# Exp tiles in column blocks of 64, one mask per unit, corner copies of V by DMA, a new order

## The chip, the cores and the metric

One core of a Trainium2 chip runs the whole kernel: TensorE (PE; PEld are its weight loads), VectorE (DVE), ScalarE (ACT), GpSimd (POOL), and SyncE (SP), which only issues DMAs here. The metric is the device time of one execution in microseconds (us); the comparison is between medians of executions.

## What is computed

Two layers, each an attention with memory (32 heads of width 16, 2,048 tokens in 4 segments of 512, causal inside a segment) and a gated feed-forward block, all in bfloat16:

```python
for s in range(N):                        # 4 segments
    logits = einsum('bhqd,bhkd->bhqk', qs, ks) * scale + mask   # causal, 512 x 512
    a_dot = einsum('bhqk,bhkd->bhqd', softmax(logits), vs)
    a_mem = (phi(qs) @ M) / (phi(qs) @ z + 1e-06)
    outs.append(g * a_mem + (1.0 - g) * a_dot)
    M, z = M + phi(ks)^T vs, z + sum(phi(ks))
x = x + A(layernorm(x)); x = x + (silu(n @ w1) * (n @ w3)) @ w2   # n = layernorm(x); twice
```

## The kernel before

The program is a list of some 3,700 operations with their dependencies. `ORDER` is a written-out permutation of their numbers; every engine runs its operations in that order and waits for the semaphores of what they depend on. `OTHER` lists the operations that take the second of two possible engines: evictions of PSUM (`ev`, L520 on ScalarE, L521 on VectorE), scalings (`km`, `ke`), sums of heads (`oadd`). There are 8 segments (4 in each layer). The attention of one segment is interleaved with the feed-forward of earlier ones and the projections of later ones.

**Logits.** The heads go in 4 groups G of 8; `ee` is the even or the odd head of a pair, and four pairs lie side by side in the array's four strips of 32 rows. One logits unit (`lg`, L984) fills 512 columns of four PSUM banks. A block `("f", G, ee, j, ...)` of a unit is row tile j (128 keys) against the queries it can see, less the first 64: widths 448, 320, 192 and 64. Those first 64 queries of each row tile (the own corner) are done for both heads at once in units of `("s", ...)` blocks. Matmuls of a unit come in groups of four, one for each strip, that run side by side. A logits unit needs row tiles; the other matmuls run with the whole array or with column tiles, and `quarters` (L233) writes a full matmul as four column tiles where it stands among attention products.

**Exp and masks.** One Exp (L1000) turns the four banks into a tile `e` of [128, 4 strips, 512]. Where a row tile meets its own diagonal, GpSimd zeroes what is above it (`affine_select`, L1009): in an `f` unit one instruction for each row tile, 128 x 256 elements; in an `s` unit four of 1,024.

**Attention product.** `attend` (L1056) multiplies V by these tiles, in four column strips; `f` blocks read V from `va`, the corners from `vj`, a copy of V with the odd heads shifted by 64 partitions (L787, two copies on VectorE for a segment, four in segment 0). There is one `vj` buffer (`VJ = 1`). The result is evicted (`evX`, tile `xs`), transposed by DMA on SyncE (L1070), normalised, and transposed back (L1101).

**The head.** Segment 0 is done in two halves, with Exp tiles of two strips. While it runs, segment 1's tokens are normalised on VectorE (L691), turned on TensorE (`flip`, L701, four flips) and evicted (L521, `W`), and segment 1's projections wait for that.

```python
for n, b in enumerate(own):
    cut(("f", n), 64, lambda ebuf=ebuf, c=b[4]: e_r[ebuf.slot][:, :, c:c + 64], [[0, 4], [1, 64]], 256)
```

Of the kernel before, what the change touches and what calls it, by code (L numbers as in the profile page):

```python
# [3 lines left out]
ACT = mybir.ActivationFunctionType  # L4
# [4 lines left out]
P = 128  # L9
# [3 lines left out]
NCG = 4  # L13
# [239 lines left out]
def o_pe(ns):  # L253
# [7 lines left out]
    27 5 30 29 0 32 31 34 33 9 35 10-13 21 2 23 1 14 36-37 44 38-39 6 15 26 45-46 16-20 40 47 41-42 48 43 49 55 54  # L261
    51 50 52 3 53 78 4 7 79 102 90 57 91-92 103-104 22 80 58 85 81-82 93 86 74 56 68 8 59-60 83 67 87-88 64 69 105
    89 94 106-110 186 96 188 187 189 61 95 97 190 111 98 191 99-100 113-114 101 84 115-119 192 120 112 121 202-203
    62 127 677 194 673 65 196 70 122-123 66 193 195 212 128 63 675 71 154 678 134 197 135-136 210 137-138 213 25
    198 200 204 76 671-672 211 139 205 140-141 199 155 124 142 129 674 156 125 143 157 201 676 130 215 158 369 159
    131 160 145 161 126 72 208 162 146 228-229 147-152 174 179-180 216 165 153 132 679 73 226 260 181-182 680 166
    175 167-168 372 370 214 227 163 261 231 373 133 218-219 362 258 176-177 266 183 217 232 259 169 687 170-172 690
    684 242 178 691 209 230 268 267 233 173 371 685 269 243 144 262 24 688 164 220 206 681 686 184 250 185 274 682
    263 251-252 275 689 272 270 1122 276-277 375 743 207 273 264 744 683 234 271 265 280 278 288-289 748-749 1120
    750-751 692 709 235 1118-1119 752 286 281 287 284 1121 710-711 253 285 712 745-746 244 1116-1117 726 279 727  # L270
    282 747 298 1123 374 376 1124 713 254-255 290 1125 704 728 283 256 300 257 705-706 299 301 308 28 729 693 221
    304 222 224 714 245 303 309-310 730 694 291 695 311 707 312 708 236 696 313 306-307 302 305 314 324 223 1127
    380 325 315 322 698 323 292 699 720 697 328 330-331 721 700 225 327 701 246 237 1126 1128 760 1129-1130 238 329
    326 248 722 702 1131 715-718 247 75 719 761 381 723 348 336 338 731 239 753 724 240 316 754 337 346 898 764 339
    377 349 732 755 334 733 378 703 763 249 734 762 756 347 382 735 1132-1133 332 351 241 335 738 333 340 1168
    1134-1135 293-294 765 1136 739 353 352 740-741 296 295 297 1169 777 1170-1171 900 383 317 742 384 1142 901 385
    318 778 757 1172 1143 350 320 319 341 321 354-355 737 902 356 781 904 1144 758 1145 1147 379 1146 782 779 736
    1163-1164 783 1148 386 1165 1149 780 342-343 367 759 77 387 1150 785 1185 388 897 389 1186 1151 784 1187 899
    390-391 903 1188 393 392 395 1166 786 1175 795 344 396 345 394 1189 787 1158 766 1159-1160 767-768 1167 789
    1176-1177 1161 796 1162 908 771 791 1197 909 1180-1181 790 1178 772 1190 1182 1191 1183 792 1192-1193 1198  # L280
    397-398 357-361 1179 1337 801 1137 1199 400 1153 399 788 793 1138-1139 401 1154 1194 797 1184 1155 802
    1156-1157 775 1140 366 776 1338 1141 799 905-906 805 794 773 769 800 407-408 798 402 774 806 770 403 809 421
# [12 lines left out]
    544 1600 890 1223 1195 1209 875 1579 1336 1601-1603 876-877 1580-1582 545 1590 1583 1224 1228 891-892 894 893
    1595-1596 551 1604 629-632 1591 1229 1597 895 1598 633-634 1599 896 1220 1226 635 1569 636-637 1570 1225 1232
    1571 1592-1594 1217 1212 1227 1233 1617 1572-1573 1618-1620 1238-1239 1621 1230 1213 1635 921 1978 926-928
    922-925 1236 1242 929 1237 1627 1234-1235 916 1638 930 1976 1605 917-919 1606-1607 1243 920 935 933 1608-1609
    1255 911 1231 1340 912-913 1240-1241 936 914 659 937 915 1628 1347 931 938 1256 1246 1629 1259 1247 1637
    647-648 934 1342-1343 649-651 932 1245 660 1258 1244 939-940 1248 661 1210-1211 662-666 1260 944 942 941 1257  # L300
    1261 1634 652 1262 943 1265-1266 945 1268 1263 667-668 1264 653-654 669 1249 1273 670 1274 1269-1270 1574-1575
    1636 1250 1576-1577 655-657 1630 1578 1982 1251-1252 1639 1584 1282 1977 1344 1631 1271 946-948 1253 658
    1585-1587 1283 952-953 1588 949 954 950-951 955 1288 1286 1980 1640 1284-1285 1289 1272 964 956 1641 965
    958-960 1642 966 1275 967 961 970 1292 968-969 1979 971-973 981 962 1287 963 974 1622-1623 982-983 1643 1276
    1293 1644 1294 1624-1625 1267 1983 1981 1984 984 1626 985 1985 1298 986 957 987 1299 1589 1295-1297 975 1987
    976-977 1277 1291 978-979 1279 1019 980 1302-1303 1989 1020 997-999 1021 988-989 1990 1003 1278 1305 1986 1022
    1000 1315 1004 1301 1290 1005 1254 990 1001 1316 991 1300 1317 1006 1002 1610 992-993 1007 1991 994-995 1306
    1319 1307 1014 1023 1015-1017 996 1611 1018 2057 1008-1010 1320 1988 1321 1011 2007 1012 1651 2008 1024 1013
    1322 1652 2009-2010 1308 1992 2018 1318 1993 2019 1280 1994-1995 1325 1655 1281 1304 1656 2011 1323 1996 1326
    1025 2020-2022 1997-1999 1026 1324 2000 1659-1660 1657 1030 1309-1310 1312 2028-2031 1633 1653 1327 1311 1654  # L310
    2001 1027 1031 1052 1032 1658 1033-1034 1313 2032 1665 1028 1661 1053 1035 2035-2037 1663 1029 2175 1054-1055
    1666 1314 2038 1036 1328-1329 2002-2004 1331 2174 2005-2006 1667 2039 1669 1664 1330 1037-1040 1670 1672
    1332-1333 2050 1662 2051-2054 1041-1042 1675 1632 1668 1047-1048 1056-1057 2045 1043 2046 2177 2047-2049 1676
    2013-2014 2176 2180 2015 1044-1045 2016-2017 1673 1049 1679-1680 1671 1674 1046 2040-2043 1050 2044 1058-1061
    2023 1677 1692-1693 2178-2179 1051 1062 1683 1363-1364 2033 1684 2181 2024-2025 1365 1358 2026-2027 1366-1367
    1694 2012 1696 1359-1361 1678 1362 1348-1349 1697 1353-1356 1374 1698 1357 1682 1350 1702 1375 1649 1068 1650
    1351 1699 1352 1685 1063 1695 1370 1069 1703 1681 1064-1065 1372-1373 1700 1371 1104 1070 1701 1705 1066 1706
    1105 1067 1368 1106-1107 1071-1074 1369 1710 1686 1376 1075-1076 1711 1108 1707 1077 1719-1720 1092-1093 1109
    1645 1377 1704 1110 1721 1379 1378 1380-1381 1078 1111 1646 1112 1079 1094 1725 1709 1726 2034 1113 2182-2183
# [103 lines left out]
def build(nc, A_x, A_wq, A_wk, A_wv, A_wo, A_beta, B_w1, B_w3, B_w2, out):  # L423
# [66 lines left out]
    def vpairs(t, i):  # L490
        return t[:, i, 0:VS * H].rearrange("p (e h c) -> p h e c", e=2, c=VS)

    def vcol(G, pg, ee):
        return VS * (16 * ee + 4 * G + pg)
# [415 lines left out]
    def unit_list(part):  # L910
# [5 lines left out]
        if part == (0, LT):  # L916
            for G in range(NCG):
# [3 lines left out]
                if G % 2 == 0:  # L921
                    out.append((share, [(G, 0)]))
# [363 lines left out]
```

## Time and profile before

| | us |
|---|---|
| median of 3 executions | 474.56 |
| lowest and highest | 474.35, 476.81 |
| the profiled execution | 477.68 |
| its span, first to last instruction | 475.9 |
| TensorE busy in the span | 461.8 |

A busy share is an average over the span; what ends a stretch is read from the timelines. A matmul's duration in the rows includes its way through the array, so distances between starts tell its cost.

### The profile page before, as it was taken

What the parts mean: (1) busy time and instruction counts of PE and PEld (TensorE: products, weight loads), DVE (VectorE), ACT (ScalarE), POOL (GpSimd) and SP (SyncE); (2) the same over time, 40 slices, a digit from 0 to 9 for tenths busy, and PEclk for the clock granted to TensorE, in tenths of its full rate; (3) what the DMA queues carried; (4) which work ended last, traced back from release to release, by engine and by line L of the source; (5) the groups of instructions that cost most, each with busy time, mean ns of one, the idle gap of its engine ahead of it and who ended that gap; (6) DMA issues with size and microseconds to landing.
All of it is one profiled execution on the core that took longest, in us unless ns stands there. A gap on an engine that the chain in (4) does not pass through costs nothing.

```text
span 475.9 us, 19641 instructions
## 1 busy us (share of the span) xinstructions
PE 461.8 (97%) x8757; PEld 237.7 (50%) x8793; DVE 388.8 (82%) x843; ACT 380.9 (80%) x362; POOL 242.3 (51%) x418
## 2 busy tenths in 40 slices
PE   8989989999999999999999999999999999999997
PEld 4544446764554444544545444454444444454554
DVE  7887998988999888798888788697795778688673
ACT  5969989999999897989888999889898887560230
POOL 3973376655565644757364533746563565550000
PEclk9979999999999999999999999999999999999999
DMA  7744637643243332281235531542315332531402
GB/s 233 273 101 59 90 72 139 155 60 68 49 77 62 68 61 37 41 113 29 45 68 70 79 68 23 68 93 45 59 25 86 28 47 46 91 81 36 102 1 69
DMA packets 105780, 35.92 MB, mean 75 GB/s; under 512 B 98816, under 2 KB 104064, under 8 KB 105696
## 3 DMA queue, kind: packets, MB, share of 16 engines
q1 hardware_dynamic: 104016, 31.41, 36.0%
q0 software_dynamic: 720, 2.46, 1.8%
q8 instruction: 69, 1.13, 1.0%
q10 hardware_dynamic: 960, 0.79, 0.5%
q14 instruction: 15, 0.12, 0.1%
HBM read 8.43 MB, written 2.10 MB: 22 GB/s over the span
## 4 chain that ended last, share of the span: by engine, by line
PE 85%; DVE 9%; ACT 3%; issue 1%; DMA 1%; POOL 0%; DVEq 0%; POOLq 0%
PE psall L228 34%; PE psall L233 33%; PE psall L984 9%; PE psall L1056 7%; ACT e L1000 2%; DVE W L521 1%; DVE xn L691 1%; DVE va L521 1%; DVE W L831 1%; DVE W L833 1%; DVE ln L672 1%; DMA x_tok<-in_A_x_dram 1%; PE psall L856 0%; DVE vj L787 0%; DVE xs L521 0%
## 5 line engine op out<-in xcount | busy, mean ns | idle before, releaser
L1000 ACT ACTIVATE e<-psall 128x2048 bf16<-128x2048 f32 (+1 forms) x162 | 272.0, 1694 | 37.3 <-PE psall L984 30.9
L1009 POOL TENSOR_SCALAR_AFFINE_SELECT e<-e 128x256 bf16<-128x256 bf16 (+2 forms) x320 | 175.2, 572 | 149.8 <-ACT e L1000 78.5
L228 PE MATMUL psall<-W,w 128*128 128x512 bf16 (+1 forms) x382 | 84.8, 352 | 0.1
L233 PE MATMUL psall<-W,w 128*32 128x512 bf16 (+1 forms) x1352 | 79.0, 361 | 0.0
L1177 DVE SCALAR_TENSOR_TENSOR gp<-th,psall 128x512 bf16<-128x512 bf16 x80 | 53.8, 681 | 12.0 <-ACT th L1175 11.4
L1181 DVE SCALAR_TENSOR_TENSOR h<-gp,psall 128x512 bf16<-128x512 bf16 x80 | 54.0, 681 | 10.7 <-PE psall L228 6.3
L1175 ACT ACTIVATE th<-psall 128x512 bf16<-128x512 f32 x80 | 47.2, 604 | 16.6 <-PE psall L233 13.8
L233 PE MATMUL psall<-w,h 128*32 128x512 bf16 (+3 forms) x916 | 54.7, 370 | 0.0
L228 PEld LDWEIGHTS psall<-W,w 128*128 128x128 bf16 x382 | 34.5, 98 | 34.5 <-issue 5.3
L233 PEld LDWEIGHTS psall<-W,w 128*32 128x32 bf16 x1352 | 33.7, 97 | 25.8 <-issue 1.7
L672 DVE BATCH_NORM_STATS2 ln<-x_tok 128x6 f32<-128x512 bf16 x64 | 42.8, 682 | 1.3 <-DMA x_tok<-in_A_x_dram 1.0
L984 PE MATMUL psall<-W,km 32*128 32x64 bf16 (+4 forms) x1056 | 38.1, 230 | 3.2 <-issue 1.3
L1056 PE MATMUL psall<-e,va 128*32 128x192 bf16 (+4 forms) x1088 | 40.0, 268 | 0.0
L521 DVE CAST W<-psall 128x512 bf16<-128x512 f32 (+1 forms) x44 | 29.5, 674 | 8.8 <-PE psall L228 4.8
L1200 DVE TENSOR_TENSOR x_tok<-psall,x_tok 128x512 bf16<-128x512 f32 (+1 forms) x33 | 21.5, 669 | 17.5 <-PE psall L233 13.3
L1093 POOL TENSOR_TENSOR og<-xg,rd 128x256 bf16<-128x256 bf16 (+1 forms) x43 | 25.6, 600 | 18.2 <-DVE rd L1087 6.2
L228 PE MATMUL psall<-w,h 128*128 128x512 bf16 (+1 forms) x124 | 31.4, 379 | 1.4 <-issue 1.1
L233 PEld LDWEIGHTS psall<-w,h 128*32 128x32 bf16 (+1 forms) x916 | 23.1, 96 | 18.5 <-issue 2.5
L1056 PE MATMUL psall<-e,vj 128*32 128x64 bf16 x1024 | 30.8, 195 | 0.8 <-DVE xs L521 0.4
L984 PE MATMUL psall<-W 16*128 16x64 bf16 (+4 forms) x544 | 30.8, 267 | 0.2
L691 DVE TENSOR_SCALAR xn<-x_tok,ln 128x512 bf16<-128x512 bf16 x64 | 26.8, 455 | 5.1 <-POOL ln L681 5.1
L984 PEld LDWEIGHTS psall<-W,km 32*128 32x128 bf16 x1056 | 15.9, 93 | 29.4 <-ACT e L1000 17.0
(98 smaller groups left out, 659.4 us busy)
## 6 DMA issues: line engine op xcount, KB each, us to landing
w<-in_B_w_dram SPq DMA_DIRECT2D x4, 688.0 KB, 8.8
out_dram<-x_tok SPq DMA_DIRECT2D x15, 128.0 KB, 1.9
w<-in_B_w_dram POOLq DMA_DIRECT2D x3, 384.0 KB, 5.0
x_tok<-in_A_x_dram POOLq DMA_DIRECT2D x2, 512.0 KB, 4.6
xg<-xs SPq DMA_TRANSPOSE x36, 3.2
W<-og SPq DMA_TRANSPOSE x36, 2.5
wk<-in_A_wk_dram SPq DMA_DIRECT2D x1, 512.0 KB, 4.3
wq<-in_A_wq_dram ACTq DMA_DIRECT2D x1, 512.0 KB, 5.8
```

The source lines that it names most:

```text
L228: return e.matmul(out, lhsT, rhs, **k)
L233: o = e.matmul(out[c:c + 32], lhsT[:, c:c + 32], rhs, tile_position=(0, c), **k)
L521: return e.tensor_copy(dst(), src())
L672: dve(lambda e: e.bn_stats(ln_r[st.slot][:, i, 0:6], x_tok[:, tt, :]), 540, reads=[("x", tt)], writes=[(st, 0, i)], bufs=[st], prio=prio, ...
L691: op = S.add([o_dve(512, False, 1.45)], lambda e, i=i, k=k, tt=tt, xn=xn: e.tensor_scalar(xn_r[xn.slot][:, k, :], x_tok[:, tt, :], ln_r[st ...
L984: o = e.matmul(S4[:, sps(pg), c:c + n], kk, q_r[z.q.slot][r, G, q0:q0 + n], start=True, stop=True, tile_position=(32 * pg, 0))
L1000: act(lambda e, N=N, ebuf=ebuf, pgs=pgs, sps=sps: e.activation(e_r[ebuf.slot][:, pgs[0]:pgs[-1] + 1, 0:N], S4[:, sps(pgs[0]):sps(pgs[-1]) ...
L1009: pool(lambda e: e.affine_select(view(), view(), pattern=pattern, compare_op=ALU.is_ge, fill=0.0, base=base, channel_multiplier=-1), n, re ...
L1056: o = e.matmul(bank(X)[32 * pg:32 * pg + 32, at:at + m], (va_r[z.va.slot] if kind == "f" else vj_r[z.vj.slot])[:, j, h:h + 32], e_r[eb.slo ...
L1175: act(lambda e, NW=NW, B=B, th=th: e.activation(th_r[th.slot][:, 0:NW], bank(B)[:, 0:NW], ACT.Tanh, scale=0.5), NW, reads=[(B, 0)], writes ...
L1177: dve(lambda e, NW=NW, B=B, th=th, gp=gp: e.scalar_tensor_tensor(gp_r[gp.slot][:, 0:NW], th_r[th.slot][:, 0:NW], 1.0, bank(B)[:, 0:NW], AL ...
L1181: dve(lambda e, NW=NW, B=B, gp=gps[fg], h=hs[fg]: e.scalar_tensor_tensor(h_r[h.slot][:, 0:NW], gp_r[gp.slot][:, 0:NW], 0.5, bank(B)[:, 0:N ...
```

## The change

- The tile `e` becomes [128, 8 column blocks, 4 strips, 64]: the four strips' blocks of 64 columns lie together. Exp writes it block by block; the attention product reads blocks of 64 columns.
- A unit's row tiles are put so that their own diagonal blocks are neighbours, and one mask covers them: 128 x 512 in segments 1 to 7, 128 x 1,024 in segment 0. For that a tile with j = 2 is cut in two pieces (64 and 128 columns), in the logits and in the attention product; in segment 0 the first row tile of each half. The four masks of an `s` unit stay, each on half of the columns and all strips. 320 masks become 184.
- `va` and `vj` are laid out with the even or odd heads outside the row tiles; the copies into `vj` become DMAs on SyncE's queue in segments 1 to 7. Segment 0 keeps its four copies on VectorE.
- `ORDER` and `OTHER` are written anew for the 3,583 operations. By the lists: the logits stand in 155 stretches on TensorE, 157 before. From ScalarE to VectorE go 7 evictions of V, 3 `km`, 1 `ke` and 1 `evX`, back go 2 evictions of K; 5 `oadd` go to VectorE, 4 halves of the normalising product to GpSimd. In front of the first eviction of a flipped tile of segment 1, VectorE no longer does two L831, one L833, one cast of `va`, one of `xs`, and the last L691, which now come behind it, nor two scalings that ScalarE does; it does two more casts of segment 0's Q, one `km` and the constants L653 and L657. The third eviction of a flipped tile stands about where it stood, the fourth some 1 us of work later and behind an L833.

```diff
-    e_r = ring("e", EN, [P, 4, 512])
+    e_r = ring("e", EN, [P, 8, 4, 64])
...
-        return VS * (16 * ee + 4 * G + pg)
+    def vcol(G, pg, ee, j):
+        return VS * (16 * (LT * ee + j) + 4 * G + pg)
...
+                        if first:
+                            dve(lambda e, dst=dst, src=src: e.tensor_copy(dst(), src()), 320 * step, mode=2.5, **k)
+                        else:
+                            S.add([("sp", 450.0, 2800.0)], lambda e, dst=dst, src=src: e.dma_start(dst(), src()), dmaq="sp", size=163840, **k)
...
+        def own(G, ee, j, split=False):
+            a, b = 128 * j + 64, 128 * t1
+            return [("f", G, ee, j, a + 64, b - a - 64), ("f", G, ee, j, a, 64)] if split else [("f", G, ee, j, a, b - a)]
+
+        corner = lambda a: [("s", a, 0, j, 128 * j, 64) for j in range(t0, t1)]
...
+                for ee in range(2):
+                    out.append((own(G, ee, 3) + own(G, ee, 0), []))
+                    out.append((own(G, ee, 2, True) + own(G, ee, 1), [(G, ee)] if ee or G % 2 else []))
...
-                        e_r[ebuf.slot][:, pgs[0]:pgs[-1] + 1, 0:N], S4[:, sps(pgs[0]):sps(pgs[-1]) + 1, 0:N], ACT.Exp, scale=SCALE),
+                        e_r[ebuf.slot][:, 0:N // 64, pgs[0]:pgs[-1] + 1, :].rearrange("p b g c -> p g b c"),
+                        S4[:, sps(pgs[0]):sps(pgs[-1]) + 1, 0:N].rearrange("p g (b c) -> p g b c", c=64), ACT.Exp, scale=SCALE),
...
+                ds = [b[4] // 64 for b in blocks if b[0] == "f" and b[5] == 128 * b[3] + 64]
+                if ds:
+                    assert ds == list(range(ds[0], ds[-1] + 1))
+                    cut("f", 64, P, ds[0], ds[-1] + 1)
+                if blocks[0][0] == "s":
+                    for a in range(2):
+                        cut(("a", a), 0, 64, 4 * a, 4 * a + 4)
+                        cut(("b", a), 64, P, 4 * a, 4 * a + 4, rd=rd + [(ebuf, ("a", a))])
...
-                    o = e.matmul(bank(X)[32 * pg:32 * pg + 32, at:at + m], (va_r[z.va.slot] if kind == "f" else vj_r[z.vj.slot])[:, j, h:h + 32],
-                                 e_r[eb.slot][:, pg, c:c + m], start=st, stop=sp, tile_position=(0, 32 * pg))
+                    o = e.matmul(bank(X)[32 * pg:32 * pg + 32, at:at + m], (va_r[z.va.slot] if kind == "f" else vj_r[z.vj.slot])[:, h:h + 32],
+                                 e_r[eb.slot][:, c // 64:(c + m) // 64, pg, :], start=st, stop=sp, tile_position=(0, 32 * pg))
```

## Rows read from the trace of the kernel before

**Rows 1.** The page's busy times: us (share of the span) x instructions.
```profile
PE 461.8 (97%) x8757; PEld 237.7 (50%) x8793; DVE 388.8 (82%) x843; ACT 380.9 (80%) x362; POOL 242.3 (51%) x418
```
**Rows 2.** A stretch: length, busy PE PEld DVE ACT POOL, clock, DMA share, GB/s.
```profile
250.00:300.00 50.00, 49.78 (x880) 23.86 (x881) 41.06 (x91) 46.99 (x45) 22.74 (x42) 1.00 0.39 61
```
**Rows 3.** Stretches of the head, TensorE alone, the same columns.
```profile
26.00:28.00 2.00, 1.59 (x58) 1.00 0.72 221
28.00:30.00 2.00, 0.73 (x20) 0.92 0.03 8
30.00:36.00 6.00, 5.61 (x59) 0.50 0.44 87
36.00:38.00 2.00, 1.95 (x16) 0.87 0.00 0
```
**Rows 4.** Timeline of TensorE in the head: start, us, what [idle before <- releaser].
```profile
27.08 0.21 PE L1056 MATMUL psall<-e,vj 128*32 128x64 bf16 x4 [0.35 <-DVE xs L521]
...
28.54 0.40 PE L701 MATMUL psall<-ident,xn 128*128 128x128 bf16 x4 [0.60 <-DVE W L521]
...
30.39 0.61 PE L984 MATMUL psall<-W,km 32*128 32x256 bf16 x4 [1.11 <-ACT e L1000]
```
**Rows 5.** A stretch of the head, VectorE alone.
```profile
18.00:32.00 14.00, 13.63 (x29) 0.92 0.40 114
```
**Rows 6.** Timeline of TensorE in the middle: two logits units and what follows.
```profile
263.41 0.41 PE L984 MATMUL psall<-W,km 32*128 32x64 bf16 x32
263.75 2.98 PE L228 MATMUL psall<-W,w 128*128 128x512 bf16 x13
266.67 0.40 PE L984 MATMUL psall<-W,km 32*128 32x448 bf16 x8
267.00 2.55 PE L228 MATMUL psall<-W,w 128*128 128x512 bf16 x11
```
**Rows 7.** Groups by line and shape: busy us, mean ns | idle before.
```profile
L1009 POOL TENSOR_SCALAR_AFFINE_SELECT e<-e 128x256 bf16<-128x256 bf16 x256 | 104.0, 428 | 132.2 <-ACT e L1000 65.9 <-DVE W L833 13.2 <-DVE mb L865 10.9
...
L1175 ACT ACTIVATE th<-psall 128x512 bf16<-128x512 f32 x80 | 47.2, 604 | 16.6 <-PE psall L233 13.8 <-PE psall L228 2.3
...
L1009 POOL TENSOR_SCALAR_AFFINE_SELECT e<-e 128x1024 bf16<-128x1024 bf16 x32 | 36.8, 1155 | 1.8 <-DVE rd L1087 0.5 <-DVE xn L691 0.4 <-DVE og L1098 0.3
...
L228 PE MATMUL psall<-w,h 128*128 128x512 bf16 x114 | 29.4, 379 | 1.4 <-issue 1.1 <-ACT xs L520 0.2
...
L228 PE MATMUL psall<-W,wq 128*128 128x512 bf16 x84 | 23.2, 380 | 0.7 <-DVE mb L865 0.6
...
L520 ACT ACTIVATE va<-psall 128x512 bf16<-128x512 f32 x13 | 7.7, 595 | 0.4 <-PE psall L228 0.4
...
L787 DVE COPY vj<-va 64x1280 bf16<-64x1280 bf16 x14 | 6.8, 489 | 0.3
```
**Rows 8.** Waits of the weight loads: us in total, times, longest.
```profile
PEld psall L1056 <- POOL e L1009: 0.5, 2, 0.3
```
**Rows 9.** DMA issues: KB each, median us to landing.
```profile
out_dram<-x_tok SPq DMA_DIRECT2D x15, 128.0 KB, 1.9
```
**Rows 10.** Timeline of VectorE in the head, up to the first flipped tile.
```profile
20.95 0.41 DVE L831 TENSOR_SCALAR W<-W 128x1024 bf16<-128x1024 bf16 x1
...
22.34 0.69 DVE L521 CAST va<-psall 128x512 bf16<-128x512 f32 x1
...
25.04 1.39 DVE L833 TENSOR_TENSOR W<-W,px 128x1024 bf16<-128x1024 bf16 x1
26.35 0.68 DVE L521 CAST xs<-psall 128x512 bf16<-128x512 f32 x1
...
27.34 0.83 DVE L691 TENSOR_SCALAR xn<-x_tok,ln 128x512 bf16<-128x512 bf16 x1
28.08 0.40 DVE L521 COPY W<-psall 128x512 bf16<-128x512 bf16 x1
```
**Rows 11.** A stretch of the head, ScalarE alone.
```profile
28.00:37.00 9.00, 5.53 (x6) 0.62 0.30 60
```

More of the change, by code (lines that the diff above doesn't have):

```diff
@@ L266 @@
[L266 to L270, printed above, removed]
@@ L930, in unit_list @@
                     if t0:
[L931 to L933 removed]
+                        out.append(([("f", G, ee, j, 128 * t0, 128 * (t1 - t0)) for j in range(t0)], []))
+                odd = own(G, 1, t0, True)
+                out.append((own(G, 0, t0, True) + own(G, 0, t0 + 1) + own(G, 1, t0 + 1) + odd[::-1], [(G, 2)] if G > HEADG else []))
                 if G == HEADG:
[L935 removed]
+                    out.append((sum((corner(a) for a in range(NCG)), []), [(a, 2) for a in range(HEADG + 1)]))
         res = []
@@ L938, in unit_list @@
             c, bl = 0, []
-            for (kind, G, ee, j, n) in blocks:
-                bl.append((kind, G, ee, j, c, n))
-                c += n
+            for b in blocks:
+                bl.append(b[:4] + (c,) + b[4:])
+                c += b[5]
             res.append((bl, done, c))
@@ L1006, in attention @@
                 rd = [(ebuf, x[0]) for x in groups]
-                def cut(key, base, view, pattern, n, rd=rd, ebuf=ebuf, pr=pr):
-                    pool(lambda e: e.affine_select(view(), view(), pattern=pattern, compare_op=ALU.is_ge, fill=0.0, base=base,
-                                                   channel_multiplier=-1), n, reads=rd, writes=[(ebuf,) + key], bufs=[ebuf], prio=pr, name="mask")
-                own = [b for b in blocks if b[0] == "f" and b[3] >= t0]
-                for n, b in enumerate(own):
-                    cut(("f", n), 64, lambda ebuf=ebuf, c=b[4]: e_r[ebuf.slot][:, :, c:c + 64], [[0, 4], [1, 64]], 256)
-                    where[("f",) + b[1:4]] = (ebuf, b[4], b[5], [(ebuf, "f", n)])
@@ L1025, in attention, with cut @@
-                for b in sh:
-                    where[("s", b[1], b[3])] = (ebuf, b[4], 64, [(ebuf, "s", a, h) for a in range(2) for h in range(2)])
+                def cut(key, base, rows, b0, b1, rd=rd, ebuf=ebuf, pr=pr):
+                    view = lambda: e_r[ebuf.slot][0:rows, b0:b1, :, :].rearrange("p b g c -> p (b g) c")
+                    pool(lambda e: e.affine_select(view(), view(), pattern=[[0, 4 * (b1 - b0)], [1, 64]], compare_op=ALU.is_ge, fill=0.0,
+                                                   base=base, channel_multiplier=-1), 256 * (b1 - b0), reads=rd, writes=[(ebuf, key)],
+                         bufs=[ebuf], prio=pr, name="mask")
@@ new lines, in attend @@
+            pieces += [("s", j) + w for j in range(t0, t1) for w in where["s", G, 0, j]]
+            meets = lambda x, y: x[5] < y[5] + y[4] and y[5] < x[5] + x[4]
+            alone = [x for x in pieces if x[1] == 0 and not any(meets(x, y) for y in pieces if y is not x)]
+            pieces = alone + [x for x in pieces if x not in alone]
+            for n, (kind, j, eb, c, m, q0, dep) in enumerate(pieces):
+                items.append((ee, j, kind, X, base + q0 - 128 * t0, eb, c, m, dep, j == 0, n < len(alone) or n == len(pieces) - 1))
@@ L1061, in attend @@
+        ncol = sum(i[7] for i in items)
         mine = [Xs[ees[0]]] if full else Xs
-        pe(av, ncol / 2.4 + 3 * len(items), mode="C", reads=[t for i in items for t in i[5][3]] + [(z.va, j) for j in range(t1)] +
+        pe(av, ncol / 2.4 + 3 * len(items), mode="C", reads=[t for i in items for t in i[8]] + [(z.va, j) for j in range(t1)] +
            [(z.vj, ee, j) for ee in ees for j in range(t0, t1)],
```

363 lines of the change are left out of this document (168 added, 195 removed), and 16 rows, old and new, of the table OTHER.

## The prediction

> **What bounds the kernel now.** I read the busy table first: TensorE is busy 97% of the span [rows 1], so what the change can give must show as TensorE time. The table by stretches then says where TensorE has room. After the first 40 us it has next to none: 49.78 of 50 us in a stretch from the middle [rows 2]. Neither the masks on GpSimd nor the corner copies on VectorE can return more there than the 0.2 us that is free in such a stretch. The exception is the head. Between 26 and 30 us TensorE works 1.59 + 0.73 of 4 us, and then its granted clock falls: 0.92, 0.50 and 0.87 in the stretches up to 38 us [rows 3]. With two levels, 1.2 and 2.4 GHz, that is (1 - 0.92) x 2 / 0.5 = 0.3, plus 6.0, plus (1 - 0.87) x 2 / 0.5 = 0.5: 6.8 us at 1.2 GHz. The idle time before it is in the timeline of TensorE: 0.35 us and 0.60 us that an eviction on VectorE ended, 1.11 us that an Exp ended [rows 4]. VectorE is busy 13.63 of the 14 us from 18 to 32 [rows 5]; the flips (PE transposes) of segment 1's tokens wait for its evictions, and with them segment 1's projections, the only large work that TensorE could do there. So two things decide: what TensorE itself has to do more or less, and whether the head is tighter.
>
> **The change part by part.** *More matmuls.* A row tile with j = 2 is now cut in two (64 masked columns, 128 others), in the logits and in the attention product, and in segment 0 the first tile of both halves too. That is 8 more groups of four side-by-side matmuls per segment and stage in segments 1 to 7, and 16 per stage in segment 0: 2 x (7 x 8 + 16) = 144 groups, 576 matmuls, 576 weight loads, with the same columns in sum. The price of a group stands in the middle of the trace. A logits unit of two groups takes 267.00 - 266.67 = 0.33 us until the next kind of work begins; a unit of eight groups with the same 512 columns takes 263.75 - 263.41 = 0.34 us [rows 6]. Six more groups for 0.01 us: 2 ns each, 144 x 0.002 = 0.3 us. That is the lower end. The upper end is a group that pays a whole place of its own: (0.34 - 0.11) / 8 = 0.029 us, 144 x 0.029 = 4.2 us, where 0.11 us is the switch of tiling worked out next. I take +0.3, since the row is the same instruction with the same 64 columns.
>
> The Trainium skill, TensorEngine Tiling (Array Packing), section Instruction Overhead, speaks against the split: each matmul carries some 60 cycles of overhead, so a free size of 1 costs as much as 60. At 2.4 GHz that is an estimate of 25 ns a group, 3.6 us for 144, against 0.3 by the row; the trace does not agree with it for groups that follow each other in one unit.
>
> *Fewer switches.* Between logits (row tiles) and other matmuls TensorE pauses. 512 columns at 2.4 GHz are 0.213 us and the unit above takes 0.33: 0.12 us to leave it. Thirteen full matmuls from 263.75 are 13 x 0.216 = 2.81 us, and the unit behind them starts at 266.67: 0.11 us to enter it [rows 6]. The new list has 155 stretches of logits instead of 157: 2 x 0.23 = -0.5 us.
>
> *Masks.* 320 instructions become 184. 256 elements take 428 ns and 1,024 take 1,155 [rows 7]; 512 must lie between, by a straight line at 670. Segments 1 to 7 save 112 x (2 x 428 - 670) = 20.8 us, segment 0 saves 8 x (4 x 428 - 1,155) = 4.5. These 25 us of GpSimd lie beside TensorE: all that its weight loads ever wait for a mask is 0.5 us in two waits [rows 8]. I take 0; the bound is -0.5. Merging delays the first of two masks by 670 - 428 = 0.24 us, but the attention product wants both, and it gets them 0.19 us sooner.
>
> *The layout of the Exp tile.* Exp now writes runs of 64 elements and the attention product reads such runs. ScalarE writes 16-element runs in 595 ns and a contiguous tile of the same size in 604; TensorE reads x in blocks of 128 with gaps in 380 ns, contiguous h in 379 [rows 7]. So 0. That no row has runs of 64 on both sides leaves a bound: 1% on each of these, some 3 us of Exp time, which the free fifth of ScalarE's time [rows 1] would cover in most places.
>
> *Corner copies by DMA.* 14 copies of 489 ns leave VectorE, 6.8 us [rows 7]; in exchange it gets ten evictions and scalings net from ScalarE, and one instruction net from GpSimd, so its load stays, and ScalarE is the one relieved. On SyncE's queue each copy is one more DMA behind transposes that wait for data. The nearest DMA with a landing time, a store of 128 KB, lands in 1.9 us [rows 9]; the copies have 160 KB, so 2 to 2.5 us, instead of 0.5. Nothing is queued behind one on VectorE any more; on SyncE the transposes of the outgoing segment are. There is one vj buffer, so a copy starts only when the last product of the segment before is done. By the list, columns counted at 2.4 GHz, 6 to 17 us of TensorE work lie between that and the first product that reads the copy, so I take 0 and keep the late case as a rival.
>
> *The head.* In front of the first eviction of a flipped tile (28.08) VectorE did six operations that the new list puts behind it: two L831 of 0.41 (one row of the two), a va cast of 0.69, L833 of 1.39, an xs cast of 0.68, L691 of 0.83 [rows 10]: 4.4 us. Two small scalings go to ScalarE; I leave them out. Five come in front instead: two casts, a scaling, two constants, which I put between 0.41 and 0.68 each by the rows of the same group: 2.0 to 3.4. So the eviction comes 1.0 to 2.4 us earlier, and the second one directly behind it. That is more than the 0.95 us that TensorE waited there. The third comes at about the same place in the list and the fourth about 1 us later, with an L833 in front of it: +0.5. If the waits go, I expect the clock to stay at 2.4 GHz. The work of 30 to 36 us, 5.61 us at half speed, and that of its edges then takes (5.6 + 0.3 + 0.5) / 2 = 3.2 us less. ScalarE bounds this: it works 5.53 of the 9 us from 28 to 37 [rows 11], so the stretch can shrink by 3.5 at most. I take -3.2; the other end is 0, when idle time of the same length only moves.
>
> **The sum.** +0.3 - 0.5 - 3.2 + 0.5 = -2.9 us. The profiled execution took 477.7 us (span 475.9 and 1.8 around it), 3.1 more than the median of the three timed runs, 474.6; its head need not be theirs to the tenth. From 477.7 the sum gives 474.8, and from the median 471.7, which I predict.
>
> **Rivals.** *The head keeps its gap (0.28).* The third and fourth flip come no earlier, so the gap moves to 30 or 32 us and the clock falls there. For it: two of four evictions are not earlier. Against it: by then segment 1's v matmuls are ready. What is left is +0.3 - 0.5 +- 1: 474.4.
> *Copies land late, slower (0.12).* In segments 2, 4 and 7 fewer than 2 us of TensorE work stand in the list between the copy and the product that reads it. If SyncE, held by the transpose ahead, issues only there, each wait is up to 1.9 + 0.5 us; three of them are 7.2 us, and with the head's gain the time is 478.9. It decides from 5.3 us of such waits upwards (2.9 that they eat and 2.4 for the limit). Against it: the transpose ahead of each has its data early.
> *Each piece pays its place (0.06).* A group costs 29 ns after all, because the weight loads of a cut tile can't hide behind only 64 columns: +4.2 - 0.3 on the sum, 475.6, and 478.3 without the head's gain. The section of the Trainium skill named above would have it so.
> *Runs of 64 cost (0.04).* Exp at 3% more is 8 us of ScalarE, and TensorE would wait for it wherever it does now: 477.
> *As forecast (0.50).* 471.7, its own range 469.5 to 473.5.
>
> **Range and chances.** Low 469.0: the head's full 3.5 us and its waits of 2.1 gone (-5.6). High 477.5: the late copies in two segments, or the split's full price. Half a per cent, 2.4 us, is about what a measurement of this kernel can tell from no change. Faster by more: most of the forecast's half and a little of the second case, 0.46. Within: 0.36. Slower: 0.18.
>
> **What would show it.** Right: granted clock 1.00 in all stretches from 6 us on; masks of 512 at 600 to 700 ns and 184 of them; logits units of three groups still at 0.33 to 0.35 us; attention products no longer than before; no VectorE copies L787 but four; no wait of TensorE for vj. Wrong: a stretch of 1.2 GHz in the head again, waits of weight loads with vj behind a DMA, Exp above 1,881 ns, or new idle time after 40 us, where the old list left almost none and the new one, which moves everything, may leave some.

## The result, and the profile after

The changed kernel takes 479.5 us (median of 12 runs, 477.6 to 483.8); the kernel before, run beside it, 477.1 (12 runs, 474.4 to 478.7; the three runs shown ahead, median 474.6, are among them). Ratio 1.0067, 95% interval 1.0038 to 1.0097: slower by 0.7%, where 0.6% faster was forecast. The profiled execution took 481.4 us. Some executions fall into a slower state, over 1.5% above the fastest of their kernel; medians and ratios here leave them out (one run of g2_shift24, two of h4_before_shift96).

The page of the changed kernel: busy times as in [rows 1], the granted clock in 40 slices of 12 us, and the queue that loads TensorE's program (packets, MB, share; the kernel before has 69 packets and 1.13 MB there).
```profile
PE 467.4 (97%) x9432; PEld 242.3 (51%) x9432; DVE 385.8 (80%) x840; ACT 374.1 (78%) x352; POOL 219.7 (46%) x281
...
PEclk9979998999999999999999999999999999999999
...
q8 instruction: 74, 1.21, 1.0%
```
Its stretches, as in [rows 3], with three more from 74 us:
```profile
core 0: us, PE busy (x) PEld busy (x) DVE busy (x) ACT busy (x) POOL busy (x), PEclk, DMA share, GB/s
26.00:28.00 2.00, 1.67 (x91) 1.12 (x88) 1.98 (x5) 1.72 (x3) 0.43 (x1) 1.00 0.78 260
28.00:30.00 2.00, 0.00 (x0) 0.00 (x0) 1.46 (x3) 0.41 (x1) 1.14 (x1) 1.00 0.80 104
30.00:36.00 6.00, 5.92 (x59) 2.33 (x63) 2.04 (x5) 3.07 (x4) 2.28 (x2) 0.56 0.28 55
36.00:38.00 2.00, 2.00 (x13) 0.66 (x12) 1.94 (x8) 2.00 (x3) 0.18 (x1) 0.60 0.00 0
74.00:76.00 2.00, 0.85 (x3) 0.33 (x4) 1.03 (x2) 2.00 (x2) 1.69 (x3) 0.79 0.90 158
76.00:78.00 2.00, 2.00 (x9) 0.90 (x8) 0.52 (x1) 0.30 (x1) 1.99 (x4) 0.50 1.06 203
78.00:80.00 2.00, 2.00 (x61) 1.07 (x63) 1.49 (x4) 0.69 (x1) 1.99 (x3) 0.86 0.70 201
```
The head still has its stretch at 1.2 GHz: 5.3 us of the six from 30 and 1.6 of the two behind, 6.9 us, as long as before. A second one, worked out the same way, is new: 0.8 + 2.0 + 0.6 = 3.4 us from 75 us. Ahead of the first, TensorE does nothing from 28 to 30 us. Its timeline, as in [rows 4], says what for:
```profile
27.43 0.20 PE L1053 MATMUL psall<-e,vj 128*32 128x64 bf16 x4
27.46 0.20 PE L1053 MATMUL psall<-e,va 128*32 128x64 bf16 x4
30.09 0.21 PE L1053 MATMUL psall<-e,vj 128*32 128x64 bf16 x4 [2.42 <-issue]
...
73.00 0.65 PE L228 MATMUL psall<-mb,W 128*128 128x128 bf16 x8
75.15 1.87 PE L228 MATMUL psall<-wo,W 128*128 128x512 bf16 x4 [1.50 <-DVE om L898]
...
91.69 0.29 PE L853 MATMUL psall<-va,W 128*32 128x34 bf16 x20
93.32 0.25 PE L853 MATMUL psall<-va,W 128*32 128x34 bf16 x12 [1.34 <-issue]
```
The waits for VectorE of [rows 4] are gone (one of 0.45 us, for an eviction on VectorE, stands ahead of 25.48 us). In their place TensorE stops for 2.42 us in the middle of one attention product, between two of its pieces. The product is one operation of the list, so the program has no wait there; "issue" means that the profile shows nothing it waited for. The stop at 92 us, inside one memory update, is of the same kind. The one at 73 us is a real wait, for the memory read on VectorE.

The operations came out as worked out (groups as in [rows 7], then the timeline as in [rows 6]):
```profile
L996 ACT ACTIVATE e<-psall 128x2048 bf16<-128x2048 f32 x126 | 236.8, 1879 | 38.5 <-PE psall L981 35.2 <-PE psall L1053 2.4
L1007 POOL TENSOR_SCALAR_AFFINE_SELECT e<-e 128x512 bf16<-128x512 bf16 x112 | 74.7, 674 | 109.1 <-ACT e L996 52.5 <-DVE W L828 12.7 <-DVE W L830 9.1
...
264.53 0.40 PE L981 MATMUL psall<-W 16*128 16x128 bf16 x12
264.86 2.13 PE L233 MATMUL psall<-W,w 128*32 128x512 bf16 x36
...
268.13 0.41 PE L981 MATMUL psall<-W,km 32*128 32x64 bf16 x32
268.48 3.84 PE L228 MATMUL psall<-W,w 128*128 128x512 bf16 x17
```
The mask of 512 takes 674 ns (670 forecast), Exp 1,879 ns, and a logits unit of three groups 0.33 us, one of eight 0.35. A full attention product, timed from its first start to the next operation's (median, 100 to 420 us), takes 0.55 us with 36 matmuls as it did with 32. No weight load or matmul waits for a copy by DMA.

### The profile page after: what moved, and what is told of

Same layout as the page of the kernel before. It is cut to its first block, busy times and chain, and to the rows that moved or that the text cites. A ratio compares the mean times of both kernels' runs of the same rounds, so it can differ in the third digit from the quotient of the medians.

```text
span 479.7 us, 20829 instructions
## 1 busy us (share of the span) xinstructions
PE 467.4 (97%) x9432; PEld 242.3 (51%) x9432; DVE 385.8 (80%) x840; ACT 374.1 (78%) x352; POOL 219.7 (46%) x281
## 3 DMA queue, kind: packets, MB, share of 16 engines
q8 instruction: 74, 1.21, 1.0%
## 4 chain that ended last, share of the span: by engine, by line
PE 88%; DVE 5%; ACT 3%; DMA 2%; issue 1%; POOL 0%
PE psall L233 35%; PE psall L228 34%; PE psall L981 9%; PE psall L1053 7%; ACT e L996 3%; DMA xg<-xs 1%; PE psall L543 1%; DMA W<-xn 1%; DVE W L514 1%; DVE xn L684 1%; DVE gp L1174 1%; PE psall L853 1%; DVE om L898 1%; PE psall L694 0%; ACT px L826 0%
## 5 line engine op out<-in xcount | busy, mean ns | idle before, releaser
L1007 POOL TENSOR_SCALAR_AFFINE_SELECT e<-e 128x512 bf16<-128x512 bf16 (+2 forms) x184 | 155.1, 858 | 158.1 <-ACT e L996 69.1
L233 PE MATMUL psall<-W,w 128*32 128x512 bf16 (+1 forms) x1432 | 81.5, 358 | 0.1
L228 PE MATMUL psall<-W,w 128*128 128x512 bf16 (+1 forms) x362 | 81.0, 354 | 0.0
L233 PEld LDWEIGHTS psall<-W,w 128*32 128x32 bf16 x1432 | 35.6, 97 | 27.7 <-issue 1.9
L228 PEld LDWEIGHTS psall<-W,w 128*128 128x128 bf16 x362 | 33.0, 98 | 31.5 <-issue 3.4
L1090 POOL TENSOR_TENSOR og<-xg,rd 128x256 bf16<-128x256 bf16 (+1 forms) x47 | 27.3, 587 | 30.6 <-DVE rd L1084 16.2
L1053 PE MATMUL psall<-e,va 128*32 128x64 bf16 (+4 forms) x1376 | 40.3, 246 | 0.5 <-DVE W L514 0.5
L514 DVE CAST W<-psall 128x512 bf16<-128x512 f32 (+1 forms) x42 | 27.7, 664 | 8.7 <-PE psall L228 7.4
L228 PE MATMUL psall<-w,h 128*128 128x512 bf16 (+1 forms) x134 | 34.0, 380 | 0.0
L1053 PEld LDWEIGHTS psall<-e,va 128*32 128x32 bf16 x1376 | 27.9, 97 | 11.2 <-DVE W L514 0.6
L228 PE MATMUL psall<-wv,W 128*128 128x512 bf16 x94 | 30.3, 398 | 1.5 <-DVE W L514 0.9
```

The costliest lines, as they stand in the source:

```text
L228: return e.matmul(out, lhsT, rhs, **k)
L233: o = e.matmul(out[c:c + 32], lhsT[:, c:c + 32], rhs, tile_position=(0, c), **k)
L514: return e.tensor_copy(dst(), src())
L1007: pool(lambda e: e.affine_select(view(), view(), pattern=[[0, 4 * (b1 - b0)], [1, 64]], compare_op=ALU.is_ge, fill=0.0, base=base, channel ...
L1053: o = e.matmul(bank(X)[32 * pg:32 * pg + 32, at:at + m], (va_r[z.va.slot] if kind == "f" else vj_r[z.vj.slot])[:, h:h + 32], e_r[eb.slot][ ...
L1090: return e.tensor_tensor(ogv()[:, 0:nt, :, k, :], src, v(1)[:, k, :, :, None].to_broadcast([P, nt, 4, DH]), ALU.mult)
```

## The experiments

All were timed beside the kernel before, whose median was 477.1 to 477.2 each time.

### Which part costs: four kernels

The order is a list of operation numbers, so it can be carried from one kernel to the other (a merged mask stands where the first of its masks stood; where masks are multiplied, they follow each other).

**e1_tiles_old_order**: the new Exp tiles, pieces and masks; V's layout, copies and order of before.
```
+    e_r = ring("e", EN, [P, 8, 4, 64])          # with own(), cut(), attend() of the change
     va_r = ring("va", 2, [P, LT, VS * H + 12])  # as before, vj by dve(shift, ...)
     ORDER = old list, merged masks counted once
```


> The new Exp tiles, the cut row tiles and the merged masks alone: V's layout, VectorE's corner copies and the order of the kernel before stay (a merged mask stands where the first of its masks stood). If the new order is to blame: within 1 us of the kernel before, since 144 more groups at 2 ns cost 0.3 us. If the cut tiles are to blame (21 more operations' worth of split matmuls apart, 576 more matmuls to fetch and issue): 2 to 4 us slower, with stalls of TensorE in the middle of a unit that wait for nothing the profile shows.

**e2_copies_old_order**: the kernel before with only the copies moved.
```
-  dve(shift, 320 * step, mode=2.5, ..., name="vj%d" % ee)
+  S.add([("sp", 450.0, 2800.0)], move, dmaq="sp", size=163840, ...)   # segments 1 to 7
```


> The kernel before with one edit: V's corner copies of segments 1 to 7 are DMAs on SyncE's queue, each at its old place in the list. If the copies are to blame (late landing, or their traffic beside instruction loading): 2 to 4 us slower, with TensorE waiting for a copy or stalled within 3 us of one. If the order or the tiles are: within 1 us of the kernel before, and no wait of a weight load for vj over 0.3 us.

**e3_both_old_order**: both edits in the old order.

> Tiles, masks and DMA copies of the change in the order of the kernel before. If the order is to blame: within 1 us of the kernel before, and 2 to 4 us below the changed kernel. If tiles and copies are to blame together: at the changed kernel's time, 2 to 4 us above the kernel before.

**e4_order_alone**: the new order on the old kernel. The new list lets a product go when the corner masks of its half are done, so the old corner masks are cut by halves of columns instead of rows of heads.
```
-  [0:64 * h + 64, 2 * a:2 * a + 2, :] ... pattern=[[0, 16], [1, 64]]
+  [0:64 * h + 64, :, 256 * a:256 * a + 256] ... pattern=[[0, 4], [0, 4], [1, 64]]
   ORDER = new list
```


> The new order with the old tiles, uncut row tiles, 320 masks (the two or four of a unit one after the other where the merged one stands) and copies on VectorE. If the order is to blame: 2 to 4 us slower than the kernel before, with TensorE idle for over 1 us near 27 and near 73 us and a second stretch of 1.2 GHz behind the latter, as in the changed kernel. If not: within 1 us. More than 4 us slower would say that the 136 extra masks or the copies stand in the way of an order that was made without them, which would blur the reading.

Measured: 483.4 us for the tiles in the old order (ratio 1.0133, 1.0109 to 1.0157), 483.7 for the copies (1.0157, 1.0125 to 1.0189), 491.3 for both (1.0293, 1.0252 to 1.0333), 482.5 for the order alone (1.0121, 1.0088 to 1.0153). Each part alone costs 5 to 7 us, both together 14, and the new order takes 12 of these back. That is more than any branch expected, except the third one of e4_order_alone. So my first theory, that one part is to blame, falls, and it looks as if a list whose order is set operation by operation fits its own program alone; the traces show this for a part of the 5 to 7 us, not for all of it. What the copies cost in a list not made for them stands in the trace of e2_copies_old_order, the queue of SyncE and then TensorE:
```profile
161.81 8.58 SPq L1108 DMA_TRANSPOSE W<-og  x2
170.43 1.27 SPq L795 DMA_DIRECT2D vj<-va  x1
...
171.18 0.39 PE L233 MATMUL psall<-W,wq 128*32 128x512 bf16 x4
174.25 0.21 PE L1063 MATMUL psall<-e,vj 128*32 128x64 bf16 x4 [2.68 <-issue]
```
The copy is issued only behind two transposes, 1.1 us before the product that reads it could start (170.43 against 171.18 + 0.39), lands 3.7 us after its issue, at 174.16 us, and the product waits 2.68 us. (A wait for a DMA can thus stand under "issue"; the product that stops at 27.7 us belongs to segment 0, whose copies are on VectorE.) That is the rival of the late copies, at its price for one place (2.4 forecast); the changed list avoids it.

Two things in these runs led on. With the old, uncut row tiles the new order has the head that was forecast, in e4_order_alone:
```profile
26.00:28.00 2.00, 1.67 (x88) 1.28 (x88) 1.86 (x5) 1.55 (x2) 1.68 (x5) 1.00 0.68 220
28.00:30.00 2.00, 2.00 (x72) 1.30 (x65) 2.00 (x5) 2.00 (x3) 1.00 (x3) 1.00 0.33 66
30.00:36.00 6.00, 5.92 (x98) 2.94 (x100) 5.71 (x14) 5.88 (x9) 3.46 (x6) 1.00 0.35 68
```
And e1_tiles_old_order and e3_both_old_order, whose TensorE runs the same matmuls at different times, stop without a wait behind the same ones. The stretches up to two such stops, first e1, then e3, with the matmuls counted in brackets:
```profile
0.00:66.80 66.80, 62.09 (x1237) 32.83 (x1237) 58.26 (x152) 57.58 (x66) 36.20 (x49) 0.97 0.60 147
0.00:76.20 76.20, 70.79 (x1490) 37.78 (x1491) 66.81 (x171) 66.30 (x75) 41.55 (x58) 0.98 0.58 141
```
```profile
0.00:68.30 68.30, 63.10 (x1237) 33.00 (x1237) 57.69 (x150) 57.53 (x66) 36.20 (x49) 0.95 0.58 146
0.00:77.95 77.95, 71.62 (x1490) 37.85 (x1491) 66.24 (x169) 66.49 (x75) 41.79 (x58) 0.96 0.56 142
```
The two stops lie 1490 - 1237 = 253 matmuls apart. On the page of the changed kernel the queue q8 brings 74 packets for 9,432 matmuls, 127 a packet (1.21 MB / 74 = 16 KB): two packets. So the second theory: TensorE runs out of program at the edge of a 16 KB piece, where the matmuls before it are short. In the changed kernel one such packet moves while TensorE stands at 27.7 us (the stretch from 27.5 to 28.6 us holds it: one packet, 5.4% of 16 engines' 1.1 us, so 0.95 us):
```profile
q1 hardware_dynamic: 468, 0.12, 60.4%
q8 instruction: 1, 0.02, 5.4%
```
The stretch behind it, up to the end of the stop, has none. Ahead of the stop at 92 us one packet moves too, and there no other transfer beside it (90.9 to 92 us):
```profile
q8 instruction: 1, 0.02, 5.3%
```
So other traffic is not needed for a stop. By their times in the trace these packets end at 28.50 and 91.87 us, and TensorE goes on at 30.09 and 93.32: 1.6 and 1.5 us that the profile does not explain. From the start of one piece to going on in the next it is 4.6 us at the first stop (25.5 to 30.09) and 3.8 at the second (89.5 to 93.32). (The starts are counted back by 127 matmuls.) f1_shift33, below, does not stop behind a piece that lasts from 22.46 to 26.62 us, 4.2 us.

The Trainium skill, Runtime: NRT & Kernel Launch, section Instruction fetch mechanics, has the program refilled in blocks of 16 KiB, 256 instructions, while it runs, and calls the cost of crossing such a boundary mostly hidden. The trace agrees with the size (127 matmuls with their weight loads are 254 instructions), but not with the cost at these two places, 2.42 and 1.34 us.

### Moving the edges

The edges can be moved with almost nothing else: the 11 warm-up matmuls at the start, on zeros, are cut into narrower ones with the same columns. n matmuls more bring every edge n matmuls earlier in the work. (The start shifts a little too: at the matmul that the changed kernel runs at 22 us, the traces of its shifted versions stand between 0.4 us ahead and 1.2 behind, and with 64 more both kernels wait for the weights wv, 1.0 and 1.2 us.)
```
   def spin(e, B=new("B"), n=1):
+      for c in range(0, 512, 512 // n):
+          o = e.matmul(bank(B)[:, c:c + 512 // n], xs_r[0][:, 0, 0:128], xs_r[0][:, 0, c:c + 512 // n], ...)
+  pe(lambda e, i=i: spin(e, n=4), ...)                                   # f1: 33 more
+  pe(lambda e, i=i: spin(e, n=16 if i < 7 else 8 if i < 8 else 1), ...)  # f2: 112 more
```


> The changed kernel; each of the 11 warm-up matmuls of 512 columns at the start is cut in four of 128 (the same columns, 33 matmuls more), nothing else. If the stall at 27.7 us is TensorE out of instructions at the edge of a 16 KB piece of its program (an edge lies at every 127.2 matmuls, here at the 474th), the edge now comes 33 matmuls earlier in the work, out of the dense stretch: no stall over 0.5 us near 27.7, no 1.2 GHz stretch behind it, VectorE's earlier evictions count, and the time falls by 3 to 6 us to 474 to 476. The stall near 92 us stays at 0.5 to 1.3. If the stall belongs to the product or to a buffer, it stays where it is, and the time stays within 1 us of the changed kernel.

> As the run before, but with 112 matmuls more in the warm-up (seven of the eleven cut in 16, one in 8): the edges lie at 489 and 1252 matmuls of the work. If TensorE runs out of instructions at edges: the head keeps a stall of 1 to 2.5 us, now at the 489th matmul of the old count, with its 1.2 GHz stretch; a new stall of about 1 us near 64 us, and the time is 0 to 2 us above the changed kernel. If the warm-up itself were what helps or harms, both shifts would go the same way.

Two more kernels complete the parts in the new order: **f3_after_vj_dve** (the change with its copies on VectorE) and **f4_order_dma** (e4_order_alone with the copies by DMA).

> The changed kernel with V's corner copies on VectorE again, each at the place of its DMA in the list. If the DMA copies are to blame for the loss: 1 to 3 us faster than the changed kernel. If the order was made for them: VectorE gets back 14 copies of 0.49 us in places where the list has no room, and it is 1 to 5 us slower than the changed kernel.

> The new order with DMA copies, but with the tiles and masks of before (576 fewer matmuls and 136 more masks than the changed kernel). If the cut tiles cost through instruction loading: no stall at 27.7 and no 1.2 GHz there, 2 to 5 us faster than the changed kernel up to 60 us. What the 136 masks cost comes on top, later, as in the run with the order alone, where up to 3 us were lost again after 320 us.

Measured: f1_shift33 474.15 us, ratio to the kernel before 0.9926 (0.9905 to 0.9948); f2_shift112 480.2 (1.0060, 1.0041 to 1.0080). The head of f1_shift33:
```profile
26.00:28.00 2.00, 1.93 (x116) 1.55 (x110) 1.96 (x5) 1.89 (x3) 0.03 (x1) 1.00 0.67 209
28.00:30.00 2.00, 1.90 (x16) 0.72 (x16) 1.45 (x4) 2.00 (x4) 1.15 (x1) 1.00 0.95 128
30.00:36.00 6.00, 6.00 (x127) 3.13 (x126) 5.90 (x18) 5.85 (x9) 4.57 (x7) 1.00 0.31 59
36.00:38.00 2.00, 1.97 (x14) 0.53 (x10) 1.93 (x6) 2.00 (x3) 2.00 (x2) 1.00 0.55 70
```
No stop, clock 1.00, and 5.3 us less than the changed kernel for 33 empty matmuls. f2_shift112 stops in the head again, 2.24 us, with 3.4 us at 1.2 GHz behind it (0.72 from 30 to 36 us). The matmuls and weight loads (the second bracket) up to the stop, in the changed kernel and in f2_shift112:
```profile
0.00:30.00 30.00, 25.68 (x474) 16.02 (x474) 25.93 (x69) 23.09 (x30) 18.80 (x26) 1.00 0.73 230
0.00:29.70 29.70, 24.37 (x598) 17.61 (x602) 25.62 (x69) 23.43 (x30) 18.84 (x26) 1.00 0.75 232
```
Four records of matmuls are missing there, so the weight loads count: 602 - 112 = 490 in the old count (489 expected). Its new stop near 64 us did not come; one of 1.62 us came at 79 us instead, behind the 1,747th weight load, 1,145 or nine pieces behind the first.

f3_after_vj_dve took 483.5 us (1.0109, 1.0083 to 1.0135), f4_order_dma 478.7 (1.0030, 1.0013 to 1.0046). In the new order the DMA copies thus give 483.5 - 479.5 = 4.0 us with the new tiles and 482.5 - 478.7 = 3.8 with the old; the tiles cost 0.8 to 1.0, place of the edges included, which is less than the runs of one kernel scatter. f4 has clock 1.00 from 28 to 36 us.

**g1_shift127** moves the edges by one whole piece, **g2_shift24** by 24; **g3_before_shift33** and **g4_before_shift104** do the same to the kernel before (the same edit, other n).

> The changed kernel with 127 matmuls more in the warm-up (eight of the eleven cut in 16, one in 8), the same columns: one whole piece of the program. If what counts is where the 16 KB edges fall, everything is back: the stall of 1.5 to 2.5 us at 27.7, the 1.2 GHz stretch behind it, and the time of the changed kernel, 479.5 within 1.5 us, although the warm-up is cut finer than in the run with 33. If cutting the warm-up helps by itself, this run is as fast as the one with 33, 474 to 475.

> As with 33, but 24 matmuls more (eight of the eleven warm-up matmuls cut in four). From the edges worked out in the trace of the changed kernel: no edge in the dense stretch before 27.7 and none at 52 us, where the run with 33 stood 0.5 us; so 474 within 1 us, at best 0.5 below the run with 33. If the stall at 27.7 stays, the edge must be moved further than the trace says: 477 to 480.

> The kernel before with the same 33 matmuls more. Its own head waits for VectorE's evictions, not for instructions, so nothing there changes, and the 1.2 GHz stretch at 30 to 36 us stays. The edge near 67 us goes (1.3 us), new ones come near 74 and 88 us (0.8 and 0.9): within 1 us of the kernel before. If 33 matmuls more helped any kernel, 3 us or more faster.

> The kernel before with 104 matmuls more, the shift at which the fewest of its edges fall into dense stretches: 1.0 to 1.5 us faster than the kernel before, 476; the head's 1.2 GHz stretch stays. So the best the old list gets from its edges is about 476, and the new list with 33 stays 1.5 to 2 us ahead of it. If the whole of the 5 us between the changed kernel and its shifted version were the edges' own, and not the head's clock, this run would be as fast as that one.

g1_shift127: 480.7 us (1.0065, 1.0041 to 1.0089). The stop is back, in the middle of a group of four, behind matmul 602 - 127 = 475, and with it the slow stretch:
```profile
0.00:31.05 31.05, 25.70 (x602) 18.38 (x602) 25.73 (x69) 23.29 (x30) 18.83 (x26) 0.99 0.68 220
...
28.64 0.19 PE L1055 MATMUL psall<-e,vj 128*32 128x64 bf16 x1
31.08 0.24 PE L1055 MATMUL psall<-e,vj 128*32 128x64 bf16 x3 [2.25 <-issue]
...
30.00:36.00 6.00, 4.92 (x50) 2.06 (x51) 1.80 (x4) 2.92 (x3) 2.23 (x3) 0.56 0.25 49
```
So the finer warm-up does nothing by itself, and the place of the edge does it.

g2_shift24: 475.8 us (0.9964, 0.9934 to 0.9995), where 474 within 1 was expected. Its four runs with a mean granted clock of 1.000 took 471.4, 472.4, 472.5 and 473.9 us; seven at 0.993 to 0.996 took 475.6 to 477.6 (the one left out, at 0.989, took 479.8, and it is the only one with a trace). At this shift one and the same program goes either way, and the two ways lie about 4.4 us apart (means 472.5 and 477.0).

g3_before_shift33 took 482.8 us (1.0105, 1.0075 to 1.0134) and g4_before_shift104 480.3 (1.0068, 1.0041 to 1.0095), where 477 and 476 were expected. Those two were wrong. In g3 the stop near 67 us is gone, as worked out, but none is seen at 88 us, the slow stretch of the head is halved (3.4 us: 0.72 from 30 to 36 us), and the time is longer. TensorE comes to its next real wait 3 us earlier and there stands longer:
```profile
73.31 0.26 PE L1058 MATMUL psall<-e,vj 128*32 128x64 bf16 x12
76.24 0.69 PE L233 MATMUL psall<-w,W 128*32 128x192 bf16 x16 [2.67 <-DMA W<-xn]
...
78.00:80.00 2.00, 2.00 (x11) 1.19 (x9) 1.37 (x3) 1.40 (x2) 0.74 (x3) 0.50 0.12 26
```
and then the clock falls there.

**h1_after_shift64, h2_after_shift96, h3_before_shift64, h4_before_shift96** complete four quarters of a piece for both kernels.

> The changed kernel with 64 matmuls more in the warm-up (half a piece). No edge in the dense stretch before 27.7 us by the trace of the changed kernel, so no 1.2 GHz stretch at 30 to 36; edges at 80 and 91 us stall 0.5 and 1.1: 474 to 477. If the place of the edges explains nothing but the two runs seen, it is anywhere from 474 to 481.

> The changed kernel with 96 matmuls more: the edge lies at the 505th matmul of the work, 1.0 us of stall at 28.2, with the 1.2 GHz stretch behind it, and 1.3 at 90: 479 to 481. If a stall in the head were harmless to the clock, 475 to 477.

> The kernel before with 64 matmuls more. With 0, 33, 64 and 96 there are four quarters of a piece for both kernels. If the change is worth its 3 us by itself and the edges only hide it, the mean of the changed kernel over the four lies 2 to 4 us below that of the kernel before; here 477 to 482, since the 1.2 GHz stretch of the head stays at every shift. If the changed kernel only had luck at 33, the means agree within 1 us.

> The kernel before with 96 matmuls more; as the run before: 477 to 482 with the head's 1.2 GHz stretch, if the change is worth its 3 us; 474 to 476 if the kernel before has lucky quarters of its own.

Measured (us, medians):
```
matmuls more     0      24     33     64     96     104    112    127
changed        479.5  475.8  474.2  481.7  481.4    -    480.2  480.7
before         477.1    -    482.8  487.3  479.4  480.3    -      -
```
At 64 the head of the changed kernel is clean, as expected (clock 1.00 from 26 to 36 us), and yet the time is not 474 to 477: compared matmul by matmul with the changed kernel's trace, it is 7.9 us ahead at 124 us and 2.2 at the end (f1_shift33 8.9 and 7.5). The waits of TensorE from 100 us on, first h1_after_shift64, then f1_shift33:
```profile
PE psall L233 <- DVE h L1180: 2.0, 2, 1.1
PE psall L228 <- DMA W<-xn: 1.0, 2, 0.7
PE psall L233 <- DMA W<-xn: 0.8, 1, 0.8
```
```profile
PE psall L228 <- issue: 1.9, 12, 0.2
PE psall L228 <- DMA W<-xn: 0.8, 1, 0.8
PE psall L233 <- DVE gp L1176: 0.6, 1, 0.6
```
(The 12 waits of f1_shift33 on "issue" are probably no waits: its record lacks 38 matmuls of L228.) At 96 TensorE does stand behind matmul 602 - 96 = 506 (505 expected), 1.51 us, but there a wait for VectorE's xn ends at the same matmul, so this stop does not tell them apart. A longer one of the same run does: 2.88 us from 80.63 us, in the middle of an attention product and on "issue", behind its 1,746th matmul, 1,144 or nine pieces further. Its packet starts to move 3.9 us after the piece before was begun (1.5 us at the stop of 92 us), while a load of x_tok and transposes move, so a packet can also come late where the piece is not that short; that the loads hold it up is not tested.

The kernel before at 64 has its slow stretch elsewhere: from 28 to 36 us its clock is 1.00,
```profile
30.00:36.00 6.00, 4.46 (x124) 2.59 (x125) 5.94 (x15) 5.16 (x6) 4.09 (x9) 1.00 0.35 97
```
and 6.8 us at 1.2 GHz lie between 12 and 24 us (0.75 and 0.68 in its two halves), where it waits for wv. Its 487.3 us are outside the 477 to 482 expected.

Over 0, 33, 64 and 96 the changed kernel's mean is (479.5 + 474.2 + 481.7 + 481.4) / 4 = 479.2 us, that of the kernel before (477.1 + 482.8 + 487.3 + 479.4) / 4 = 481.7: 2.5 apart, as expected, but the four differences run from -8.6 to +2.4, too wide apart to call the mean shown.

## Why the prediction was wrong

**The step that failed** is the head: "If the waits go, I expect the clock to stay at 2.4 GHz." The waits for VectorE went and the clock fell all the same, because a stop of 2.42 us that I had no price for stood in the same place. It is TensorE's own program arriving late at the edge of a piece: the stop moves with the edge (490 with 112 more, 475 with 127 more), is gone with 33 more, and the slow stretch goes with it. In the traces with the new order, those that stop in the head (the changed kernel, f2, f3, g1 and h2, for 1.51 to 2.42 us) have 3.4 to 6.9 us at 1.2 GHz behind it; those that do not (e4, f4, f1, h1) have none. The one trace of g2_shift24 has a wait of 0.86 us and 3.4 us at 1.2 GHz. The prediction had the end 0 for the case that idle time of the same length only moves; this is that case, but by another cause than the rival "the head keeps its gap", which looked for it in the third and fourth flip.

**The dependency part of that step was right.** The first flipped tile is evicted at 24.72 us in the changed kernel instead of 28.08, 3.4 us earlier where 1.0 to 2.4 were worked out. With the stop moved away nothing in the head waits over 0.25 us from 24 to 36 us, the clock is 1.00, and f1_shift33 is 477.2 - 474.15 = 3.1 us faster than the kernel before; the sum said 2.9. That the two agree so well is in part luck, since with 64 more the head is as clean and the time is 481.7. Of the 7.8 us between the forecast (471.7) and the result (479.5), 2.5 are the kernel before itself, which took 477.1 in more runs than the three that I started from (474.6); the other 5.3 are what f1_shift33 takes back (479.5 - 474.15). From 477.1 the sum would have given 474.2, still 5.3 below the result. By the traces f1_shift33 is 5.7 us ahead of the changed kernel at 40 us. Further on, the matmuls behind the memory update start at 93.40 us in the changed kernel and at 86.31 in f1_shift33, 7.1 us earlier: the first stop and half of its slow stretch can give 2.4 + 6.9 / 2 = 5.8 of it, the rest is the second slow stretch and a shorter stop.

**Extra matmuls (+0.3).** Right as a price per group (0.33 us for a unit of three, as of two before [rows 6]); no piece pays its place, in the logits or in the attention product. (The prediction's 25 ns a group were added to columns that take 64 / 2.4 = 27 ns by themselves; the units show 2 ns.) But the pieces are also instructions: 9,432 matmuls instead of 8,793 (of which [rows 1] shows 8,757), five packets more of program. 576 of the 639 are the pieces; the other 63 come with the new order, which alone has 8,856 (e4_order_alone). Groups of 64 and 128 columns use a packet up fast: from 25.48 to 27.66 us, 2.2 us, in the changed kernel's head. I counted columns and starts, and not the supply.

**Switches, masks, Exp layout, copies (-0.5, 0, 0, 0).** Nothing in the runs speaks against them: 674 ns, 1,879 ns, no wait for a copy. The copies by DMA are worth more than I gave them: 3.8 to 4.0 us in the new order, probably since 14 copies are off VectorE, on which the list counts.

**After 40 us** I had written that a list which moves everything may leave new idle time, and gave it no term. It left 1.50 us at 73, 1.34 at 92, 0.55 and 0.91 at 114 and 120 us, and 3.4 us at 1.2 GHz. The wait at 73 us comes with the order: e4_order_alone has it too, 2.41 us. The one at 92 us is an edge, 1,873 - 474 = 1,399 matmuls or eleven pieces behind the first.

**What stays open.** Why the lead of the head is nearly kept at 33 and given back after 124 us at 64. What passes in the 1.5 us between the end of a packet and TensorE's going on. Why every shifted version of the kernel before is slower than the unshifted one; g3 shows one way (the time gained is waited away and the clock falls), not the reason for all four. What decides at 24 more matmuls, run by run, which way it goes. And so what the change is worth apart from the place of its edges: the best of the seven changed versions (median 474.15 us) beats the best of the five old ones (477.1); that much is measured, and a best of several is in part chance.

## What to carry to other kernels

A change of the instruction count moves every place where TensorE's program is fetched in pieces; before a result of one per cent is put down to the edit, run it with the edges moved (empty instructions at the start do it), for both kernels. When TensorE stops in the middle of an operation and the profile names nothing, count the matmuls up to there and compare with the packets of the instruction queue. An order set by hand is made for one program: a part of a change tried in the old order is measured together with its misfit (here +6 and +7 us).

## What was not expected of the hardware

TensorE's program arrives in 16 KB packets while it runs, about one for 127 matmuls, and each takes about 1 us to move (0.95 and 0.93 us at the two stops). Where 127 matmuls last 2.2 us, TensorE stood up to 2.4 us for it. One idle stretch of that length was followed by 6.9 us at 1.2 GHz, one of 2.24 us in f2_shift112 by 3.4; runs of one program with the mean clock at 1.000 and just below it lay 4.4 us apart.
